# Attention and mixer kernel: the last part put in program order instead of the scheduler's order

## The chip, the cores and the metric

The kernel runs on one core of a Trainium2 chip. A core has five engines that each work through a queue of their own and wait for each other by semaphores: TensorE (PE, with the weight loads shown apart as PEld), VectorE (DVE), ScalarE (ACT), GpSimd (POOL) and SyncE (SP). DMA queues move data between the device's memory and the core. The metric is the device time of one execution in microseconds (us).

## The reference

Inputs are `q`, `k`, `v` (8 batches, 8 heads, 576 positions, 64 elements), `s` (8, 8, 576), and the weights `U` (576 x 32), `V` (32 x 576), `w_ch1` (512 x 2048) and `w_ch2` (2048 x 512). All is float32; the kernel works in bfloat16 with float32 sums.

```python
scores = scale * np.matmul(q, k.transpose(0, 1, 3, 2))
cum = np.cumsum(np.maximum(s, 0.0), axis=-1)
bias = -(cum[:, :, :, None] - cum[:, :, None, :])
scores = np.where(causal, -1000000000.0, scores + np.minimum(bias, 0.0))
attn = softmax(scores)                       # over the last axis
x = np.matmul(attn, v)                       # heads side by side: (8, 576, 512)
h = x.transpose(0, 2, 1) @ U @ V             # low-rank mixing along the sequence
u = x + h.transpose(0, 2, 1)
out = u + np.maximum(u @ w_ch1, 0.0) @ w_ch2
```

## The kernel before

The 64 pairs of batch and head are taken two heads at a time: 32 head pairs n = 0 to 31, four to a batch. For one head pair there are these pieces of work.

- `place(g)` prepares two head pairs (group g): DVE turns the loaded `qk_sd` by four transposes (line 172), and SP issues one DMA for the bias rows (line 164) and eight for the turned data (line 177) into one of three slots. It stands two head pairs ahead of the scores that use it.
- `scores(n)` multiplies k and q on PE (line 205), 18 matmuls into seven score tiles, ACT takes the exponential (lines 219, 227, 231, 235), and DVE cuts the part above the diagonal by a minimum with a mask (line 198). The bias is in the matmul, by four more rows of q and k.
- `values(n)` multiplies by v for each of the two heads (15 matmuls, line 261); DVE then takes the reciprocal of the row sums (line 270) and multiplies into the tile `x_sb` (line 271).
- `mix(n)` is the sequence mixer. Five matmuls with U (line 286) write columns 0 to 127 of the tile `up`; DVE casts them to `ux` (line 295). Four matmuls (line 298) and one (line 306) copy x in transposed form by an identity, and two (lines 315 and 318) add V times `ux`. Line 306 writes columns 128 to 191 of `up`, the tile that line 295 reads. DVE copies the sums into `uT` (lines 326 and 327).
- `widen(g)` and `narrow(g)` are the two halves of the FFN over 512 tokens. A step of `widen` is four matmuls of 512 columns (line 339) and a RELU on ACT (line 346). A step of `narrow` is four matmuls of 512 columns (line 355); each fourth step adds four matmuls that add u (line 366), a copy of the sum on DVE (line 375) and a DMA to the output (line 376).

The FFN steps are a list, `fill`. `run(gen, rate)` takes a piece of work from one `yield` to the next and after each takes `rate` steps from the list. `attend(n, rate)` runs `scores(n)`, `values(n - 1)` and `mix(n - 1)` in this way: four, two and one yields. So the text of the program has an FFN step after each part of the scores, after each head of `values`, and after the first ten matmuls of `mix`.

`opening()` does batch 0, `second()` batch 1 with a rate of 0.4, and `rest()` the other batches with a rate of 1.0, then the FFN steps that are left. Nothing is in the list during `attend(8)`: `widen(1)` is put into it after that pair.

The order in which each engine meets its instructions is set in two ways. Within `tc.manual_schedule()` it is the order of the program's text. Outside it, the framework's own scheduler orders the instructions of each engine by priorities and by what it expects to be ready, and it may pull an instruction ahead of others that the program has first. `opening()` and `second()` lie within, `rest()` outside.

Matmul results go to two pools of four PSUM tiles: `ps_s` for scores, `ps_w` for all others. `qk_sd` has three buffers, `turned` and `x_sb` two, `o_sb` three.

Of the kernel before, what the change touches and what calls it, by code (L numbers as in the profile page):

```python
# [20 lines left out]
def kernel(  # L21
# [81 lines left out]
    def load_qk(g):  # L103
        qk_t[g] = loads.tile([128, 2, ST * D], BF16, tag="qk_sd", name="qk_sd", bufs=3)
        for c, src in enumerate((q, k)):
            for a in range(4):
                nc.gpsimd.dma_start(  # L107
                    out=qk_t[g][ds(32 * a, 32), c, :].rearrange("p (n f) -> p n f", n=6),
                    in_=src[g // 2, 4 * (g % 2) + a].rearrange("(n p t) d -> p n (t d)", p=32, t=3),
                )  # L110

    def load_v(b):
        vt = v_slots[b % 3]
        for t in range(4):
            nc.gpsimd.dma_start(  # L115
                out=vt[:, t, :, 0:D],
                in_=v[b, :, ds(t * 128, 128), :].rearrange("h p d -> p h d"),
            )
        nc.gpsimd.dma_start(
            out=vt[:64, 4, :, 0:D], in_=v[b, :, 512:576, :].rearrange("h p d -> p h d")  # L120
        )
# [40 lines left out]
    def place(g):  # L162
        slot = slots[g % NSLOT]
        nc.sync.dma_start(
            out=slot[D:KA, :, 0 : 2 * S],
            in_=rows_hbm[:, ds(4 * g, 4)].rearrange("r n c s -> r n (c s)"),
        )
        src = qk_t.pop(g)
        turned = work.tile([128, 2, 2, S], BF16, tag="turned", name="turned")
        for e in range(2):  # L170
            for c in range(2):
                nc.vector.transpose(  # L172
                    turned[:, e, c].rearrange("p (n m t) -> p n t m", n=6, t=3),
                    src[:, c].rearrange("p (n t e d) -> p e n t d", n=6, t=3, e=2)[:, e],
                )
            for a in range(4):
                nc.sync.dma_start(
                    out=slot[ds(32 * e, 32), a, 0 : 2 * S],
                    in_=turned[ds(32 * a, 32), e].rearrange("p c s -> p (c s)"),
                )  # L180
# [153 lines left out]
    def widen(g):  # L334
        hT = hidden[g] = work.tile([128, NF, 512], BF16, tag="hT", name="hT")
        for nf in range(NF):
            f1 = pwork()
            for kt in range(4):
                nc.tensor.matmul(  # L339
                    f1,  # L340
                    lhsT=w1_sb[nf // 4][:, kt, ds(nf % 4 * 128, 128)],
                    rhs=uT[:, kt, ds(g * 512, 512)],
                    start=(kt == 0),
                    stop=(kt == 3),
                )
            nc.scalar.activation(hT[:, nf, :], f1, RELU)  # L346
            yield

    def narrow(g):
        hT = hidden.pop(g)  # L350
        for i in range(4):
            f2 = pwork()
            tok = g * 512 + i * 128
            for nf in range(NF):
                nc.tensor.matmul(  # L355
                    f2,
                    lhsT=hT[:, nf, ds(i * 128, 128)],
                    rhs=w2_sb[nf // 4][:, nf % 4, :],
                    start=(nf == 0),
                    stop=False,  # L360
                    skip_group_check=True,
                )
                if nf % 4 == 3 and nf < NF - 1:
                    yield
            for dt in range(4):
                nc.tensor.matmul(  # L366
                    f2[:, ds(dt * 128, 128)],
                    lhsT=uT[:, dt, ds(tok, 128)],
                    rhs=identity,
                    start=False,  # L370
                    stop=(dt == 3),
                    skip_group_check=True,
                )
            o_sb = work.tile([128, DM], FP32, tag="o_sb", name="o_sb", bufs=3)
            nc.vector.tensor_copy(o_sb, f2)  # L375
            nc.sync.dma_start(out=out_flat[ds(tok, 128), :], in_=o_sb)
            yield
# [4 lines left out]
    def step_fill():  # L382
        while fill:
            if next(fill[0], fill) is not fill:
                return
            fill.pop(0)
# [19 lines left out]
    def attend(n, rate):  # L406
        b, hp = divmod(n, PB)
        if n < NP:
            run(scores(n), rate)
        if n > PB:  # L410
            run(values(n - 1), rate)
            run(mix(n - 1), rate)
            if hp == 0:
                fill.append(widen(b - 1))
# [117 lines left out]
    def second():  # L532
        fill.append(widen(0))
        place(2)
        fill_with(6)
        load_qk(4)
        load_v(2)
        for i in range(3):
            load_w2(i)
        load_qk(5)  # L540
        load_w2(3)
        attend(4, 0.4)
        place(3)
        attend(5, 0.4)
        attend(6, 0.4)
        place(4)
        attend(7, 0.4)
        fill_with(16)

    def rest():  # L550
        for n in range(2 * PB, NP + 1):
            b, hp = divmod(n, PB)
            if hp == 0 and b + 1 < B:
                load_qk(2 * b + 2)
                load_qk(2 * b + 3)
                load_v(b + 1)
            if hp % 2 == 0 and n // 2 + 1 < NP // 2:
                place(n // 2 + 1)
            attend(n, 1.0)
            if n == 2 * PB:  # L560
                fill.append(narrow(0))
            if hp == 0:
                fill.append(narrow(b - 1))
        fill.append(widen(NG - 1))
        fill.append(narrow(NG - 1))
        while fill:
            step_fill()

    with tc.manual_schedule():
        opening()  # L570
        second()
    rest()


# [28 lines left out]
```

## Time and profile before

| | |
|---|---|
| median of 3 runs | 425.99 us (425.75 to 426.89) |
| the profiled execution | 425.99 us, of which span 423.9 us |
| PE busy | 386.5 us (91%) |
| DVE, ACT, POOL busy | 198.2, 191.9, 111.4 us |
| mean granted PE clock | 0.954 |
| HBM read, written | 37.51 MB, 9.95 MB |

The span is the time from the first to the last instruction of the program; the execution takes some 2 us more around it. "Busy" is the time that an engine has an instruction in work. A matmul is drawn for longer than it holds the next one back, so PE can look busy while it waits a little. A line of a timeline has its start, its length, the engine, the line of the program, the operation, what it writes and reads, how many instructions are merged, and in brackets the engine's idle time before it with what ended that.

### The profile page before, as it was taken

What the parts mean: (1) busy time and instruction counts of PE and PEld (TensorE: products, weight loads), DVE (VectorE), ACT (ScalarE), POOL (GpSimd) and SP (SyncE); (2) the same over time, 40 slices, a digit from 0 to 9 for tenths busy, and PEclk for the clock granted to TensorE, in tenths of its full rate; (3) what the DMA queues carried; (4) which work ended last, traced back from release to release, by engine and by line L of the source; (5) the groups of instructions that cost most, each with busy time, mean ns of one, the idle gap of its engine ahead of it and who ended that gap; (6) DMA issues with size and microseconds to landing.
All of it is one profiled execution on the core that took longest, in us unless ns stands there. A gap on an engine that the chain in (4) does not pass through costs nothing.

```text
span 423.9 us, 8293 instructions
## 1 busy us (share of the span) xinstructions
PE 386.5 (91%) x3252; PEld 220.4 (52%) x3308; DVE 198.2 (47%) x433; ACT 191.9 (45%) x375; POOL 111.4 (26%) x179
## 2 busy tenths in 40 slices
PE   6794786769999999999999999999999999999996
PEld 2473343545555556555555655566555444444442
DVE  7565443779667685655747443344434101001011
ACT  3362463645652334773376337743770260440620
POOL 8566753295851850620030000000000000000000
PEclk9579868988999999999999999999999999999999
DMA  7999999899993996892291221001000201102001
GB/s 112 155 139 111 198 157 193 114 179 159 170 128 108 193 154 124 85 103 79 64 120 29 73 65 56 2 26 51 26 2 25 76 0 51 49 0 76 26 26 74
DMA packets 78573, 37.93 MB, mean 89 GB/s; under 512 B 64518, under 2 KB 69798, under 8 KB 78534
## 3 DMA queue, kind: packets, MB, share of 16 engines
q0 software_dynamic: 67312, 18.44, 52.7%
q1 hardware_dynamic: 11222, 18.96, 15.3%
q8 instruction: 26, 0.43, 0.4%
q14 instruction: 13, 0.11, 0.1%
HBM read 37.51 MB, written 9.95 MB: 112 GB/s over the span
## 4 chain that ended last, share of the span: by engine, by line
PE 65%; DMA 19%; POOL 6%; DVE 4%; issue 3%; SPq 1%; DVEq 0%; POOLq 0%
PE pwork L355 26%; PE pwork L339 23%; DMA w_sb<-in_moe_w_ch_dram 6%; PE pscore L205 6%; DMA v_slot<-in_v_dram 5%; PE pwork L261 4%; DMA qk_sd<-in_k_dram 4%; DMA qk_sd<-in_q_dram 3%; DVE turned L172 3%; POOL qk_sd L107 3%; PE pwork L286 2%; PE pwork L366 2%; POOL v_slot L115 2%; PE pwork L315 1%; DMA slot<-turned 1%
## 5 line engine op out<-in xcount | busy, mean ns | idle before, releaser
L339 PE MATMUL pwork<-uT,w_sb 128*128 128x512 bf16 x548 | 143.8, 390 | 1.8 <-issue 0.4
L355 PE MATMUL pwork<-w_sb,hT 128*128 128x512 bf16 x552 | 138.1, 379 | 1.2
L346 ACT ACTIVATE hT<-pwork 128x512 bf16<-128x512 f32 x144 | 87.7, 610 | 112.3 <-PE pwork L339 112.2
L205 PE MATMUL pscore<-slot 68*128 68x128 bf16 (+4 forms) x576 | 71.8, 254 | 10.9 <-DMA slot<-turned 6.4
L339 PEld LDWEIGHTS <-w_sb 128*128 128x128 bf16 x576 | 52.5, 100 | 52.4 <-issue 7.7
L355 PEld LDWEIGHTS <-hT 128*128 128x128 bf16 x576 | 51.3, 97 | 47.8 <-issue 1.8
L219 ACT ACTIVATE pT<-pscore 128x512 bf16<-128x512 f32 x64 | 38.8, 606 | 76.1 <-PE pscore L205 62.4
L375 DVE COPY o_sb<-pwork 128x512 f32<-128x512 f32 x36 | 24.8, 689 | 96.7 <-PE pwork L366 96.6
L205 PEld LDWEIGHTS <-slot 68*128 68x128 bf16 x576 | 44.9, 104 | 43.0 <-issue 12.7
L172 DVE STREAM_TRANSPOSE turned<-qk_sd 128x576 bf16<-128x576 bf16 x56 | 58.6, 1116 | 0.8 <-DMA slot<-turned 0.4
L198 DVE TENSOR_TENSOR pT<-pT,keep 128x512 bf16<-128x512 bf16 (+1 forms) x84 | 27.4, 350 | 48.7 <-ACT pT L219 44.4
L227 ACT ACTIVATE pT<-pscore 128x512 bf16<-128x512 f32 x64 | 39.0, 610 | 12.0 <-PE pscore L205 11.9
L261 PEld LDWEIGHTS <-pT 128*128 128x128 bf16 x960 | 37.4, 99 | 11.6 <-issue 0.2
L107 POOL DMA_DIRECT2D qk_sd<-in_q_dram x56 | 31.7, 580 | 32.4 <-DVE pT L198 19.5
L261 PE MATMUL pwork<-v_slot,pT 128*128 128x65 bf16 x960 | 40.0, 195 | 0.0
L115 POOL DMA_DIRECT2D v_slot<-in_v_dram x32 | 28.2, 898 | 42.9 <-PE pwork L261 42.0
L231 ACT ACTIVATE pT<-pscore 128x512 bf16<-128x512 f32 x64 | 39.4, 616 | 0.0
L107 POOL DMA_DIRECT2D qk_sd<-in_k_dram x56 | 31.6, 573 | 26.0 <-DMA w_sb<-in_moe_w_ch_dram 13.2
L326 DVE CAST uT<-pwork 128x512 bf16<-128x512 f32 x31 | 21.3, 688 | 23.4 <-PE pwork L318 23.4
L271 DVE TENSOR_TENSOR x_sb<-pwork,rec 128x320 bf16<-128x320 f32 x64 | 31.2, 488 | 1.9
L286 PE MATMUL pwork<-x_sb,U_sb 128*128 128x128 bf16 x160 | 14.6, 223 | 13.4 <-DVE x_sb L271 13.3
L270 DVE RECIPROCAL rec<-pwork 128x5 f32<-128x5 f32 x64 | 12.0, 188 | 26.3 <-PE pwork L261 26.2
(61 smaller groups left out, 186.7 us busy)
## 6 DMA issues: line engine op xcount, KB each, us to landing
out_dram<-o_sb SPq DMA_DIRECT2D x36, 256.0 KB
slot<-turned SPq DMA_DIRECT2D x112, 72.0 KB
v_slot<-in_v_dram POOLq DMA_DIRECT2D x32, 128.0 KB, 6.4
w_sb<-in_moe_w_ch_dram POOLq DMA_DIRECT2D x8, 512.0 KB, 8.2
qk_sd<-in_q_dram POOLq DMA_DIRECT2D x56, 72.0 KB, 5.5
qk_sd<-in_k_dram POOLq DMA_DIRECT2D x56, 72.0 KB, 4.4
v_slot<-in_v_dram POOLq DMA_DIRECT2D x8, 64.0 KB, 7.0
rows_hbm<-hT SPq DMA_DIRECT2D x1, 504.0 KB
```

The costliest lines, as they stand in the source:

```text
L107: nc.gpsimd.dma_start(out=qk_t[g][ds(32 * a, 32), c, :].rearrange("p (n f) -> p n f", n=6), in_=src[g // 2, 4 * (g % 2) + a].rearrange("(n ...
L115: nc.gpsimd.dma_start(out=vt[:, t, :, 0:D], in_=v[b, :, ds(t * 128, 128), :].rearrange("h p d -> p h d"),)
L172: nc.vector.transpose(turned[:, e, c].rearrange("p (n m t) -> p n t m", n=6, t=3), src[:, c].rearrange("p (n t e d) -> p e n t d", n=6, t= ...
L205: nc.tensor.matmul(dst, lhsT=kT[:, ds(j * 128, 128)], rhs=qT[:, lo:hi], start=start, stop=stop, skip_group_check=not stop,)
L219: nc.scalar.activation(pT[:, hh, 0:512], diag, EXP, scale=scale)
L227: nc.scalar.activation(pT[:, hh, 512:1024], far, EXP, scale=scale)
L231: nc.scalar.activation(pT[:, hh, 1024:1536], mid, EXP, scale=scale)
L261: nc.tensor.matmul(po[:, i, :], lhsT=pT[:, hh, ds(spot(j, i), 128)], rhs=vt[:, j, h, :], start=(j == 0), stop=(j == i), skip_group_check=True,
L271: nc.vector.tensor_tensor(x_sb[:, :, ds(h * D, D)], po[:, :, 0:D], rec.to_broadcast([128, 5, D]), op=ALU.mult,)
L339: nc.tensor.matmul(f1, lhsT=w1_sb[nf // 4][:, kt, ds(nf % 4 * 128, 128)], rhs=uT[:, kt, ds(g * 512, 512)], start=(kt == 0), stop=(kt == 3),)
L346: nc.scalar.activation(hT[:, nf, :], f1, RELU)
L355: nc.tensor.matmul(f2, lhsT=hT[:, nf, ds(i * 128, 128)], rhs=w2_sb[nf // 4][:, nf % 4, :], start=(nf == 0), stop=False, skip_group_check=True,
```

## The change

The call of `rest()` is moved into the block of `tc.manual_schedule()`. All instructions of batches 2 to 7 and of the FFN after them then stand on every engine in the order of the program's text. No instruction is added, removed or altered.

```diff
     with tc.manual_schedule():
         opening()
         second()
-    rest()
+        rest()
```

## The prediction

> **What bounds the kernel now.** I read the page's busy times first, then busy time by stretch, then the tensor engine's (PE's) timeline around one mixer step, and last the vector engine's (DVE's) where PE waits longest.
>
> ```profile
> PE 386.5 (91%) x3252; PEld 220.4 (52%) x3308; DVE 198.2 (47%) x433; ACT 191.9 (45%) x375; POOL 111.4 (26%) x179
> PE   6794786769999999999999999999999999999996
> ```
>
> PE is the bound. Its idle time lies in the first quarter, up to about 106 us. Busy time by stretch (columns: us, then busy time of PE, PEld, DVE, ACT, POOL with instruction counts, granted clock, DMA, GB/s) says the same:
>
> ```profile
> 83.30:104.00 20.70, 14.94 (x127) 8.96 (x126) 18.05 (x35) 9.21 (x20) 14.12 (x23) 0.84 1.60 165
> 100.00:326.00 226.00, 221.44 (x2115) 131.41 (x2153) 127.49 (x294) 117.44 (x234) 49.91 (x79) 1.00 0.58 84
> 326.00:420.00 94.00, 93.53 (x472) 44.33 (x478) 9.68 (x14) 28.66 (x48) 0.00 (x0) 1.00 0.11 40
> ```
>
> From 100 us on PE has almost nothing to win: the reader should see 221.4 of 226 us and, in the tail, 93.5 of 94. So a new order of the same instructions can win only what is left of waits, and loses whatever PE waits it opens. Busy time hides part of a wait, because a matmul is drawn longer than its issue distance (512 columns are drawn 0.38 us and follow each other every 0.215). I therefore count a wait as the distance between two starts less the usual distance. PE's timeline around three mixer steps (start, us, what, idle before):
>
> ```profile
> 174.42 1.03 PE L339 MATMUL pwork<-uT,w_sb 128*128 128x512 bf16 x4
> 175.28 0.22 PE L205 MATMUL pscore<-slot 68*128 68x128 bf16 x1
> 175.41 0.45 PE L286 MATMUL pwork<-x_sb,U_sb 128*128 128x128 bf16 x5
> 175.70 0.39 PE L298 MATMUL pwork<-identity,x_sb 128*128 128x128 bf16 x4
> 175.93 0.38 PE L339 MATMUL pwork<-uT,w_sb 128*128 128x512 bf16 x1
> 176.25 0.19 PE L306 MATMUL pwork<-identity,x_sb 128*128 128x64 bf16 x1
> 176.28 0.81 PE L339 MATMUL pwork<-uT,w_sb 128*128 128x512 bf16 x3
> ...
> 194.38 0.45 PE L286 MATMUL pwork<-x_sb,U_sb 128*128 128x128 bf16 x5
> 194.67 0.39 PE L298 MATMUL pwork<-identity,x_sb 128*128 128x128 bf16 x4
> 195.22 0.19 PE L306 MATMUL pwork<-identity,x_sb 128*128 128x64 bf16 x1 [0.16 <-DVE ux L295]
> ```
>
> L306 writes into the tile that the cast L295 still reads, so it waits for that cast. Where L306 follows L298 at once it starts 0.55 us after it instead of 0.23: a wait of 0.32. Where the scheduler put one FFN matmul between (175.93), L306 starts 0.32 after that one instead of 0.215: a wait of 0.107.
>
> **The change, part by part.** Nothing is added or removed; every instruction from batch 2 on is put in the order in which `rest()` issues it. I compared the two built programs' orders. On PE, before, each of the 24 mixer steps of pairs 8 to 31 mostly stands as nine matmuls (five L286, four L298), FFN matmuls, L306, FFN matmuls, L315 and L318, with one score matmul or an extra FFN matmul ahead of L286. After, all 24 stand as ten in a row, then one FFN step, then L315 and L318, with just one FFN step between the last L261 and L286.
>
> *L306.* Before, in the stretch from 100 to 326 us: 15 of the 24 wait 0.107, two 0.32, one 0.36, one 0.205, five nothing: 2.8 us. After: the ten in a row put all 24 at 0.32 or more. For five pairs (10, 14, 18, 22, 26) a FFN output tile ends in the step just before L286, and the DVE order then is L375 (its copy), then L295. L375 starts 0.20 after the last L366, holds the next DVE instruction back 0.60 and L306 starts 0.34 after L295 starts: 1.14, of which the nine matmuls cover 0.51; 0.63 is left. So 19 x 0.323 + 5 x 0.63 = 9.3. That is **+6.5**. Bounds: -0.2 if every one waits only the 0.107 of the row at 175.93, +8.8 if the five wait 1.1 each. I take the bare row, because all 24 will stand as it does.
>
> *L286 waits for x_sb (L271).* From 100 us on these waits add up to 3.5 us before; 2.6 of it are four long ones (0.40, 0.55, 1.35, 0.32) behind a transpose L172 or copy L375 that the scheduler placed among L270 and L271. After, no L172 stands there. But only one FFN step covers reciprocal and multiply: at 315.93 such a step is followed by L286 0.98 later, 0.863 of it work, a wait of 0.12. 19 such pairs give 2.3 (in the other five the step has four L366 more and covers all).
> The four L172 of a `place` now stand together ahead of the pair's L198, L270. From the end of L318: 0.17 to the copies, 0.71 for L326 and L327, 4 x 0.98 for L172, 0.8 for three L198: the first L270 can start at 5.6 us. PE needs 1.37 for the scores, 4 x 0.86 for FFN steps, 0.45 for L261 and 0.23 to DVE: 5.5. The second L270 is due 1.3 later, so the lateness is made good; with one or two L375 (0.6 each) ahead of it some 0.5 us in all remain. Sum 2.8: **-0.7**. Bounds: -3.5 (all such waits gone) to +6 (0.6 more in each of 10 pairs with `place` in this stretch, less what went).
>
> *The start of `rest()`, 83 to 104 us.* DVE there, before:
>
> ```profile
> 84.85 0.18 DVE L270 RECIPROCAL rec<-pwork 128x5 f32<-128x5 f32 x1
> 84.95 1.09 DVE L172 STREAM_TRANSPOSE turned<-qk_sd 128x576 bf16<-128x576 bf16 x1
> 85.89 0.48 DVE L271 TENSOR_TENSOR x_sb<-pwork,rec 128x320 bf16<-128x320 f32 x1
> 86.27 0.19 DVE L270 RECIPROCAL rec<-pwork 128x5 f32<-128x5 f32 x1
> 86.37 1.09 DVE L172 STREAM_TRANSPOSE turned<-qk_sd 128x576 bf16<-128x576 bf16 x1
> 87.30 0.47 DVE L271 TENSOR_TENSOR x_sb<-pwork,rec 128x320 bf16<-128x320 f32 x1
> ...
> 87.83 0.72 PE L286 MATMUL pwork<-x_sb,U_sb 128*128 128x128 bf16 x5 [4.33 <-DVE x_sb L271]
> ```
>
> Two transposes of `place(5)` were pulled up into the middle of this chain, and PE waits 4.33 us. After, they stand behind L327, so L286 can start at about 86.0 (1.8 earlier). Next, scores(8) needs the slot that `place(4)` fills. Its last L177 is issued at 86.7, as now; at the two earlier places scores began 3.8 and 4.0 us after the last L177, so 90.6, against 91.19 now. Then the gain is lost again: pair 8 has no FFN step to fill with, since widen(1) is queued only after it. So 0.9 for L261, bare, waits for DVE, where `place(5)`'s L172 run from 88.9 to 92.8 and L198 waits for the last exponential (about 94.2): L286 of pair 7 at about 95.9 against 97.34. Before, the scheduler had by then also done scores(9) (1.37 us). Up to L261 of pair 8 come 0.85 + 0.25 for the mixer, 1.37 for scores(9), 3.45 for four FFN steps: 101.8. Before it starts at 103.93 with nine more matmuls of scores(10) done (0.68), so 103.25 like for like: a gain of 1.4 if the clock stays full, 0 if another 3.4 us go at half clock. I take **-0.8**; bounds 0 and -2.7 (slots land by 88.8, full clock).
>
> The clock rows of this stretch:
>
> ```profile
> 84.40:87.80 3.40, 0.00 (x0) 0.00 (x0) 3.40 (x10) 0.00 (x0) 3.28 (x6) 1.00 0.86 138
> 87.80:91.20 3.40, 3.14 (x16) 1.81 (x18) 2.16 (x3) 0.27 (x1) 3.10 (x6) 0.50 1.27 195
> 94.70:98.10 3.40, 2.44 (x22) 1.60 (x23) 3.40 (x9) 3.26 (x8) 1.10 (x3) 0.99 2.69 148
> 98.10:101.50 3.40, 3.40 (x14) 1.59 (x14) 3.40 (x8) 0.00 (x0) 1.09 (x2) 0.50 1.99 155
> ```
>
> A wholly idle 3.4 us is followed by 3.4 us at 0.50, but so is a stretch with PE drawn busy 2.44 of 3.4 us. The Trainium skill (TensorE: Matmul & The Clock Gate, Part 1) has the clock halved after one idle window of about 3.4 us. By that rule none of the new waits (2.6 us at most) would halve it, this step would be -1.4 instead of -0.8 and the sum 430.4; the row at 98.1 speaks against relying on it.
>
> *Other queues.* SP's copies L376 now stand ahead of the `place` that follows them in the program; each waits for a L375 that is ahead of that place's L172 on DVE too, so SP holds nothing up. Slots: L172 done 5 us into a pair, eight L177 at 0.6, 4 to land: 14 us, and the slot is wanted two pairs (19 us) later. POOL's order is the same but for one load of v, six pairs before its use; its loads start later, as qk_sd comes free later, with some six pairs in hand. ACT needs about 7 us of each 9.5. The last 94 us have the same order in both. All cost nothing unless a pair's time fell to 14/2 = 7 us.
>
> **Sum.** 6.5 - 0.7 - 0.8 = +5.0 us. The profiled execution took 425.99 us, its span 423.9 and 2.1 around it; it is also the median of the three shown. Forecast **431.0 us** (+1.2%).
>
> **Rivals.**
> 1. *Faster: the freed DVE chain outweighs.* The long x_sb waits go (4.33 at 83.3 and the four later ones). Priced at its best: -2.7 at the start, -3.5 at L286. It decides only if the L306 waits come to less than 6.2 us more, under 0.375 each; at 0.215 each (+2.4) the time is 426.0 + 2.4 - 6.2 = 422.2. Against it: the trace has seven bare places at full clock, each with 0.32. 6%.
> 2. *Four L172 in a row make every second pair late.* If L198 and L375 between them push L270 past 1.3 us of slack, each of ten pairs loses 0.6 more, +6: 437. For it: DVE has 7.6 us of work in such a pair of 9.5. Against: the slack above. 10%.
> 3. *No change that shows.* Start at -2.7 and L306 at +4 (the five without their copy, some more hidden): 426 to 427.3. 6%. That the change does nothing is excluded, the orders differ on PE from pair 8 on.
>
> **How the numbers follow.** My forecast's case, 428 to 434, has 78%. A measurement here tells about 0.3% (1.3 us) from no change. The low end takes the start at -2.7, L286 at -1.4 and the five copies at no cost (-1.5): +0.9 to +1.4, so 427.4; the high end adds 3.5 of rival 2's 6 us: 434.5. Faster 6%, within 0.3% 6%, slower 88%.
>
> **What would show it.** In the profile after: L306's group waits for ux in 20 or more places, 0.16 us each as drawn; the waits of L286 over 1 us gone after 100 us; L286 of pair 6 near 86 us; PE's busy share unchanged in the last 94 us; span near 429. Wrong would be: L306 not waiting (then rival 1), or DVE idle-free in every second pair with L286 waiting 0.5 us and more (rival 2).

## The result and the profile after

| | median | ratio to before, 95% interval |
|---|---|---|
| before | 425.87 us | |
| after | 431.9 us | 1.013 (1.0092 to 1.0168) |
| after, measured again later | 432.11 us (before: 426.05) | 1.0126 (1.009 to 1.0161) |

The change makes the kernel 6 us slower, between 4 and 7 by the interval; 5.0 were forecast. The profiled execution of after took 429.94 us (span 428.2), the fastest of its four, against 423.9 of span before. Its first 82 us, which hold the same instructions in both kernels, happened to be 1.0 us quicker. Counted from the second head of pair 6's values (the L261 at 82.88 before, 81.90 after) to the end it is 341.1 us before and 346.3 after: 5.2 us more, like for like.

The page of after, busy times and PE in 40 slices, then busy time by stretch:

```profile
PE 387.3 (90%) x3251; PEld 219.3 (51%) x3308; DVE 198.7 (46%) x433; ACT 191.8 (45%) x375; POOL 111.4 (26%) x179
PE   6695796659999999999999999999999999999996
```

```profile
83.30:104.00 20.70, 14.23 (x145) 9.13 (x148) 12.04 (x31) 9.58 (x20) 13.20 (x21) 0.92 1.39 142
100.00:326.00 226.00, 218.45 (x2088) 128.76 (x2126) 129.20 (x294) 117.95 (x237) 48.20 (x76) 1.00 0.53 82
330.00:424.00 94.00, 93.47 (x471) 44.38 (x479) 9.69 (x14) 28.66 (x48) 0.00 (x0) 1.00 0.11 40
```

The work is the same, instruction by instruction. In the stretch from 100 to 326 us PE is busy 3 us less and so gets less done; the last 94 us are as before. The 40 slices hide it, since each still shows a 9: what was lost is many small waits. PE's timeline around two mixer steps shows the two sizes that they have:

```profile
113.85 0.45 PE L286 MATMUL pwork<-x_sb,U_sb 128*128 128x128 bf16 x5
114.14 0.39 PE L298 MATMUL pwork<-identity,x_sb 128*128 128x128 bf16 x4
114.68 0.19 PE L306 MATMUL pwork<-identity,x_sb 128*128 128x64 bf16 x1 [0.16 <-DVE ux L295]
114.71 1.02 PE L339 MATMUL pwork<-uT,w_sb 128*128 128x512 bf16 x4
...
123.30 0.39 PE L366 MATMUL pwork<-identity,uT 128*128 128x128 bf16 x4
123.52 0.44 PE L286 MATMUL pwork<-x_sb,U_sb 128*128 128x128 bf16 x5
123.80 0.39 PE L298 MATMUL pwork<-identity,x_sb 128*128 128x128 bf16 x4
124.66 0.19 PE L306 MATMUL pwork<-identity,x_sb 128*128 128x64 bf16 x1 [0.48 <-DVE ux L295]
```

At 114 us L306 starts 0.54 us after the first L298 where four such matmuls take 0.22: 0.32 us lost. At 123.5 us it starts 0.86 after: 0.64 lost. DVE's timeline says why the second is longer: the copy L375 stands ahead of the cast L295 that L306 waits for.

```profile
123.72 0.69 DVE L375 COPY o_sb<-pwork 128x512 f32<-128x512 f32 x1 [0.36 <-PE pwork L366]
124.33 0.28 DVE L295 CAST ux<-pwork 128x128 bf16<-128x128 f32 x1
```

Among all waits this is one line (us in total, times, longest us). Before had the first of these two, after has the second, with four times as much:

```profile
PE pwork L306 <- DVE ux L295: 1.5, 9, 0.2
PE pwork L306 <- DVE ux L295: 6.5, 31, 0.5
```

Measured as starts less usual distance, pairs 8 to 31 lose 19 x 0.32 and 5 x 0.64 us here, 9.3 in all.

At the start of `rest()` the transposes no longer split the chain of pair 6. PE there:

```profile
85.27 0.45 PE L286 MATMUL pwork<-x_sb,U_sb 128*128 128x128 bf16 x5 [2.75 <-DVE x_sb L271]
...
87.24 0.86 PE L205 MATMUL pscore<-slot 68*128 68x128 bf16 x9
88.33 1.36 PE L205 MATMUL pscore<-slot 68*128 68x128 bf16 x9 [0.24 <-ACT pT L219]
89.53 1.08 PE L261 MATMUL pwork<-v_slot,pT 128*128 128x65 bf16 x30
94.19 0.61 PE L286 MATMUL pwork<-x_sb,U_sb 128*128 128x128 bf16 x5 [3.58 <-DVE x_sb L271]
```

The wait of 4.33 us is 2.75 now. But pair 7, which has no FFN step to fill with, waits 3.58 us for DVE, which does `place(5)`'s four transposes first:

```profile
88.15 4.02 DVE L172 STREAM_TRANSPOSE turned<-qk_sd 128x576 bf16<-128x576 bf16 x4
92.02 0.85 DVE L198 TENSOR_TENSOR pT<-pT,keep 128x512 bf16<-128x512 bf16 x3
...
93.64 0.49 DVE L271 TENSOR_TENSOR x_sb<-pwork,rec 128x320 bf16<-128x320 f32 x1
```

### The profile page after: what moved, and what is told of

Its sections match the earlier page's. It is cut to its first block, busy times and chain, and to the rows that moved or that the text cites. A ratio compares the mean times of both kernels' runs of the same rounds, so it can differ in the third digit from the quotient of the medians.

```text
span 428.2 us, 8269 instructions
## 1 busy us (share of the span) xinstructions
PE 387.3 (90%) x3251; PEld 219.3 (51%) x3308; DVE 198.7 (46%) x433; ACT 191.8 (45%) x375; POOL 111.4 (26%) x179
## 4 chain that ended last, share of the span: by engine, by line
PE 73%; DMA 15%; DVE 5%; POOL 4%; issue 2%; SPq 0%; DVEq 0%; POOLq 0%
PE pwork L355 28%; PE pwork L339 26%; PE pscore L205 8%; DMA w_sb<-in_moe_w_ch_dram 7%; PE pwork L261 5%; DMA hT<-in_k_dram 2%; PE pwork L366 2%; PE pwork L286 2%; DMA slot<-turned 2%; DMA v_slot<-in_v_dram 2%; DVE ux L295 2%; POOL v_slot L115 1%; DVE turned L172 1%; DMA qk_sd<-in_q_dram 1%; DVE o_sb L375 1%
## 5 line engine op out<-in xcount | busy, mean ns | idle before, releaser
L355 PE MATMUL pwork<-w_sb,hT 128*128 128x512 bf16 x549 | 136.7, 379 | 1.4
L205 PE MATMUL pscore<-slot 68*128 68x128 bf16 (+4 forms) x576 | 69.9, 253 | 11.7 <-DMA slot<-turned 6.3
L375 DVE COPY o_sb<-pwork 128x512 f32<-128x512 f32 x36 | 24.8, 688 | 97.4 <-PE pwork L366 97.4
L172 DVE STREAM_TRANSPOSE turned<-qk_sd 128x576 bf16<-128x576 bf16 x56 | 56.5, 1115 | 0.2 <-issue 0.2
L261 PEld LDWEIGHTS <-pT 128*128 128x128 bf16 x960 | 37.2, 99 | 11.4
L261 PE MATMUL pwork<-v_slot,pT 128*128 128x65 bf16 x960 | 39.5, 195 | 0.0
L271 DVE TENSOR_TENSOR x_sb<-pwork,rec 128x320 bf16<-128x320 f32 x64 | 31.5, 492 | 2.2
L286 PE MATMUL pwork<-x_sb,U_sb 128*128 128x128 bf16 x160 | 14.6, 222 | 12.4 <-DVE x_sb L271 12.2
L286 PEld LDWEIGHTS <-U_sb 128*128 128x128 bf16 x160 | 9.5, 98 | 22.0 <-DVE x_sb L271 17.9
```

What stands on the lines that cost most here:

```text
L172: nc.vector.transpose(turned[:, e, c].rearrange("p (n m t) -> p n t m", n=6, t=3), src[:, c].rearrange("p (n t e d) -> p e n t d", n=6, t= ...
L205: nc.tensor.matmul(dst, lhsT=kT[:, ds(j * 128, 128)], rhs=qT[:, lo:hi], start=start, stop=stop, skip_group_check=not stop,)
L261: nc.tensor.matmul(po[:, i, :], lhsT=pT[:, hh, ds(spot(j, i), 128)], rhs=vt[:, j, h, :], start=(j == 0), stop=(j == i), skip_group_check=True,
L286: nc.tensor.matmul(up[:, 0:128], lhsT=U_sb[:, t, :], rhs=x_sb[:, t, cols], start=(t == 0), stop=(t == 4), skip_group_check=True,)
L355: nc.tensor.matmul(f2, lhsT=hT[:, nf, ds(i * 128, 128)], rhs=w2_sb[nf // 4][:, nf % 4, :], start=(nf == 0), stop=False, skip_group_check=True,
```

## The experiments

Each edit is shown against the kernel named. Times are medians. The kernel before, run beside each session, took 425.67 us with E1 to E4, 425.65 with E5 to E8 and 426.05 with E9 to E11.

Single executions of one kernel lie some us apart, and much of that arises in the first 100 us. The long stretch can be compared more sharply: from the first L286 of pair 8 to the end of the span, where the granted clock is 1.00 in all these profiles up to the last microsecond. After and its repetition E10 agree there within 0.1 us, though their spans are 2.4 us apart.

| kernel | L286 of pair 8 starts | span | from there to the end |
|---|---|---|---|
| after | 104.28 | 428.2 | 323.9 |
| E10, after again | 106.69 | 430.6 | 323.9 |
| E1 | 107.53 | 422.1 | 314.6 |
| E3 | 103.31 | 427.2 | 323.9 |
| E4 | 110.60 | 442.5 | 331.9 |
| E5 | 107.38 | 422.0 | 314.6 |
| E6 | 105.42 | 418.2 | 312.8 |
| E7 | 109.37 | 431.4 | 322.0 |
| E8 | 104.64 | 426.6 | 321.9 |

### E1 and E2: L306 ahead of L286

```diff
         up = pwork()
+        if n >= 2 * PB:
+            tail_of_x()          # the matmul of line 306, start=True
         for t in range(5):
             nc.tensor.matmul(up[:, 0:128], ..., start=(t == 0), ...)
...
-        nc.tensor.matmul(up[:, 128:192], lhsT=x_sb[:, 4, cols], ..., start=True, ...)
+        if n < 2 * PB:
+            tail_of_x()
```

E1 does this to after, E2 to before. The cut is shortened: `tail_of_x()` is a function that holds the one matmul of line 306.

> Kernel after, with the matmul of L306 issued ahead of the five of L286 for pairs 8 to 31 (in the code: for n >= 8). Theory (the wait of L306 for the cast L295 is the loss): 24 such waits, 9.3 us in the profile of after, are gone; the next to need the cast is L315, 1.39 us after the first of the ten, and the cast is done by 1.14 at the latest, so no new wait; L286's waits for x_sb stay as they are. Span 428.2 - 9.3 = 419, time 431.9 - 9.3 = 422.6 us, faster than before (0.992). Rival (the pairs are paced by the vector engine's chain, and PE only meets the next wait): under 3 us less, 429 us or more.

> Kernel before (scheduler's order in the last part), with the same move of L306. Theory: only the 2.8 us that such waits cost in before can go: 425.9 - 2.8 = 423.1 us (0.993), so that with and without the scheduler the kernel is within 1 us once this wait is gone. Rival (the scheduler's order is worth more than that elsewhere): this kernel is faster than the one with program order by 3 us or more, 419 to 420 us.

In both kernels a part of the computation is lost and the output is another one. The likely reason is that a start flag of L286 now comes behind L306 on the same tile, so that x of the last 64 positions of a batch does not reach u (last section). The number and size of the instructions are the same.

E1: **422.86 us**, 0.9934 (0.9911 to 0.9957), where 422.6 was expected. No wait of L306 for the cast is left, and the waits for x_sb, now at the moved matmul, are as in after (2.5 us from 100 us on). From L286 of pair 8 to the end the profile is 9.3 us shorter than after, which is the sum of the waits that were taken away. The loss of the change is this wait; nothing else takes its place.

E2: 423.68 us, 0.9955 (0.9924 to 0.9985), expected 423.1. So far with and without the scheduler look alike once the wait is gone: from the second head of pair 6's values to the end both profiles have 338.6 us. Of these the granted clock was 0.50 for 13.7 us in E1 and for 6.8 in E2, so this agreement says little of the order itself; E11 comes back to it.

### E3: `place(5)` behind pair 8

```diff
-            if hp % 2 == 0 and n // 2 + 1 < NP // 2:
+            if n > 2 * PB and hp % 2 == 0 and n // 2 + 1 < NP // 2:
                 place(n // 2 + 1)
             attend(n, 1.0)
+            if n == 2 * PB:
+                place(n // 2 + 1)
```

> Kernel after, with place(5) issued after head pair 8's work instead of ahead of it. Theory (place(5)'s four L172 hold x_sb of pair 7): L286 of pair 7 starts near 92.2 us instead of 94.2, since only the last exponential and L198 stand before it; 1.9 us gained there. The slot for scores(10) then lands at 102.5 to 105 us, and scores(10) is due at 102.7, so up to 2.3 us are given back there: time 430 to 432 us. Rival (the wait at pair 7 has another cause, such as the exponentials or the clock): L286 of pair 7 stays at 93.7 us or later.

429.66 us, 1.0093 (1.0058 to 1.0128): 2.2 less than after, but the two intervals overlap. The profile is clearer. In it the distance from L286 of pair 6 to L286 of pair 7 is 7.19 us where after has 8.92, 1.7 less, near the 1.9 of the theory; from L286 of pair 8 on it is as long as after. PE:

```profile
87.40 0.45 PE L286 MATMUL pwork<-x_sb,U_sb 128*128 128x128 bf16 x5 [2.74 <-DVE x_sb L271]
...
94.59 0.44 PE L286 MATMUL pwork<-x_sb,U_sb 128*128 128x128 bf16 x5 [1.86 <-DVE x_sb L271]
...
105.27 0.42 PE L205 MATMUL pscore<-slot 68*128 68x128 bf16 x5
```

scores(10) at 105.27 waits for nothing, so the part that was to be given back was not. The absolute times that were expected are missed by 2 us, since this execution reached pair 6 that much later. In this execution the clock gained too. After, the stretch behind the wait of 3.58 us ran at half clock, here the stretch behind a wait of 1.86 us did not (columns as above; the first two rows are after, the third is E3):

```profile
90.90:94.30 3.40, 0.11 (x2) 0.11 (x2) 3.17 (x9) 0.00 (x0) 3.40 (x7) 1.00 2.17 163
94.30:97.70 3.40, 3.18 (x20) 2.05 (x20) 1.54 (x4) 0.60 (x1) 1.63 (x4) 0.50 2.21 141
```

```profile
94.60:98.00 3.40, 3.24 (x29) 2.02 (x29) 2.44 (x5) 1.58 (x4) 0.06 (x1) 1.00 1.65 97
```

That is not the edit's doing for sure. E6 below has the same edit and the same wait of 1.86 us, and in its profile the stretch behind it did run at half clock (the wait lies in the first row):

```profile
93.28:96.69 3.41, 1.39 (x18) 1.01 (x18) 1.98 (x7) 0.31 (x3) 0.79 (x2) 1.00 2.10 126
96.69:100.10 3.41, 3.41 (x11) 1.42 (x10) 3.41 (x6) 2.15 (x4) 0.00 (x0) 0.50 0.05 1
```

The Trainium skill (TensorE: Matmul & The Clock Gate, Part 1) has the clock halved after one idle window of about 3.4 us. The rows of after and of E3 agree with that. E6's row, with PE busy for 1.39 us, does not, and neither does the prediction's row at 94.70. So the measurements go beyond that rule, and what decides the clock after a short wait stays open.

### E4: one more transpose in each place

```diff
-            for c in range(2):
+            for c in ([0]*1 if e == 0 and g > 4 else []) + [0, 1]:
                 nc.vector.transpose(turned[:, e, c]..., src[:, c]...)
```

> Kernel after, with one of the four transposes L172 of each place from place(5) on done twice (the output is the same). It takes 0.98 us more on the vector engine in each of 11 places. In after the second L270 of such a pair waits 0.42 us for PE where no L375 stands ahead of it, and not at all where one does. Theory (that is all the slack there is): 0.56 us more in about five pairs, 0.98 in about five, 0.98 in pair 8: +8 us, 440 us. Rival (the four transposes are well covered, as the forecast had it with 1.3 us of slack): +1 to +2, 433 to 434 us.

442.28 us, 1.039 (1.0348 to 1.0432): 10.4 over after, more than the 8 of the theory and far from the 1 to 2 of the forecast's cover. From L286 of pair 8 to the end the profile is 8.0 us longer than after, close to the 7.7 that the theory has for the ten pairs there. The rest lies ahead of that, where the granted clock was 0.50 for 10.2 us in this execution and for 3.4 in after. In its timeline DVE runs without a break from the copies to the second L271 of a pair with a copy, and PE waits:

```profile
133.58 5.22 DVE L172 STREAM_TRANSPOSE turned<-qk_sd 128x576 bf16<-128x576 bf16 x5
138.66 0.72 DVE L198 TENSOR_TENSOR pT<-pT,keep 128x512 bf16<-128x512 bf16 x2
139.30 0.68 DVE L375 COPY o_sb<-pwork 128x512 f32<-128x512 f32 x1
...
140.88 0.49 DVE L271 TENSOR_TENSOR x_sb<-pwork,rec 128x320 bf16<-128x320 f32 x1
```

```profile
141.42 0.45 PE L286 MATMUL pwork<-x_sb,U_sb 128*128 128x128 bf16 x5 [0.87 <-DVE x_sb L271]
```

The four transposes fit in after, but only just: of the 0.98 us of a fifth some 0.2 are covered in the mean of the ten pairs.

### E5: the wait taken away with the computation kept

```diff
             nc.tensor.matmul(up[:, 0:128], ..., start=(t == 0), ...)
+        nc.tensor.matmul(
+            up[:, 128:192], lhsT=x_sb[:, 4, cols], rhs=identity[:, :64],
+            start=False, stop=False, skip_group_check=True,
+        )
         ux = work.tile([128, 128], BF16, tag="ux", name="ux")
         nc.vector.tensor_copy(ux, up[:, 0:128])
...
-        nc.tensor.matmul(up[:, 128:192], ..., start=True, stop=False, ...)
```

> Kernel after, with L306 issued right behind the five matmuls of L286 and ahead of the cast L295, without a start flag of its own (the one of L286 opens the tile for it), in every pair. Theory: the same 9.3 us as in the run with L306 ahead of L286 go from pair 8 on, and a few tenths before; 422 to 423 us, ratio to before 0.992. Rival (that run was quicker because a part of the computation was lost, not because of the wait): 428 us or more.

**422.9 us**, 0.993 (0.9904 to 0.9956): the same as E1, and 314.6 us from L286 of pair 8 on as there, so E1's time does not come from what it lost. PE's timeline, where L294 is the moved matmul and L306 now the four that were L298; this is the step that waited 0.64 before:

```profile
125.76 0.39 PE L366 MATMUL pwork<-identity,uT 128*128 128x128 bf16 x4
125.98 0.44 PE L286 MATMUL pwork<-x_sb,U_sb 128*128 128x128 bf16 x5
126.26 0.19 PE L294 MATMUL pwork<-identity,x_sb 128*128 128x64 bf16 x1
126.29 0.39 PE L306 MATMUL pwork<-identity,x_sb 128*128 128x128 bf16 x4
126.51 1.03 PE L355 MATMUL pwork<-w_sb,hT 128*128 128x512 bf16 x4
```

With this one matmul moved, program order is faster than both kernels of the case.

### E6 and E7: two FFN steps ahead of the mixer

```diff
                 op=ALU.mult,
             )
-            yield
+            if n < 2 * PB or hh == 1:
+                yield
+            if n >= 2 * PB and hh == 1:
+                yield
```

E7 is after with this edit alone; E6 has it together with those of E5 and E3.

> The kernel of the run before, with two more edits: place(5) behind pair 8's work, and from pair 8 on both FFN steps of the values part behind its second head, so that two steps and not one cover reciprocal and multiply ahead of L286. Theory (terms add up): 422.9 - 2.2 (place(5)) - 2.5 (19 waits of 0.12 and two of 0.26 at L286) = 418.2 us, ratio 0.982. Rival (PE then meets a wait that they hid, such as for a PSUM tile): 421 us or more.

> Kernel after, with only the second of these edits: from pair 8 on both FFN steps of the values part stand behind its second head. Theory: L286's waits after 100 us (2.5 us in the profile of after) go, L306's stay: 429.4 us. Rival (they are a part of the same chain and come back at L306): no change, 431 to 432 us.

E7: 429.96 us, 1.0104 (1.0063 to 1.0145), 1.9 under after, 2.5 expected. The intervals overlap, but the profile is 1.9 us shorter from L286 of pair 8 on. There L286 waits in one place only, 0.08 us, and L306 as in after (19 times 0.32, 5 times 0.64). The two waits are separate. A part of the gain is lost at a new wait. These are all of PE's waits from 100 us on that show as idle time (L309 is what was L306):

```profile
PE pwork L309 <- DVE ux L298: 5.4, 24, 0.5
PE pwork L261 <- DVE uT L329: 0.3, 1, 0.3
```

E6: **418.9 us**, 0.9842 (0.9808 to 0.9876), expected 418.2. The terms add up: E5's time less what E3 and E7 gained (2.2 and 1.9) is 418.8. From 100 us on PE hardly waits:

```profile
100.00:316.00 216.00, 215.68 (x2134) 129.83 (x2133) 128.44 (x296) 118.60 (x237) 52.69 (x84) 1.00 0.58 90
```

### E8: the copy of the FFN's sums on ACT

```diff
-            nc.vector.tensor_copy(o_sb, f2)
+            nc.scalar.copy(o_sb, f2)
```

> Kernel after, with the copy of the FFN's sums (L375) on the scalar engine in place of the vector engine. Theory: the five waits of 0.64 at L306, where that copy stands ahead of the cast, become 0.32, and the two of 0.26 at L286 become 0.12: 1.9 us less, 430 us. Rival (another reason for the five): they stay at 0.64.

428.88 us, 1.0075 (1.0048 to 1.0101), 3.0 under after, 1.9 expected; from L286 of pair 8 on the profile is 2.0 us shorter, so the rest is within the spread. All 24 waits of L306 are 0.32 now, the step with L366 among them, which settles what the five were:

```profile
123.65 0.39 PE L366 MATMUL pwork<-identity,uT 128*128 128x128 bf16 x4
123.88 0.44 PE L286 MATMUL pwork<-x_sb,U_sb 128*128 128x128 bf16 x5
124.16 0.39 PE L298 MATMUL pwork<-identity,x_sb 128*128 128x128 bf16 x4
124.70 0.19 PE L306 MATMUL pwork<-identity,x_sb 128*128 128x64 bf16 x1 [0.16 <-DVE ux L295]
```

### E9 to E11: the scheduler once more

E9 is before with E5's edit, E10 is after unchanged, E11 is E6 with `rest()` outside the manual schedule:

```diff
         second()
-        rest()
+    rest()
```

> Kernel before (scheduler's order in the last part), with L306 right behind the five of L286 and no start flag of its own, the whole computation kept. Theory: 2.8 us of waits at L306 go, as in the run with L306 ahead: 423 to 424 us (0.995). Rival (the earlier run was quicker for the part of the computation that it lost): 425.9 us, no change.

> Kernel after, unchanged, in the same session as the other two, since its four runs lay 2.7 us apart. Theory: 431 us, 1.2% above before; if the median were under 430, the gains put on place(5), on the two steps and on the copy would be smaller by that much.

> The kernel with all three edits, but with rest() outside the manual schedule, in the scheduler's hands. Theory (once the waits are gone the two orders differ only at the start of rest(), where the scheduler pulls transposes into the chain of pair 6 but does scores(9) early): within 1.5 us of the 418.9 us with program order. Rival (the scheduler's order costs something of its own in the long stretch): 421 us or more.

E10 gave 432.11 us, so the comparisons with after stand. The other two went against the theory. E9: 426.33 us, 0.9987 (0.9959 to 1.0015), where 423 to 424 was expected: no gain that can be told. (Its interval overlaps E2's, so that it gains less than E2 is not certain either.) E11: 423.12 us, 0.9924 (0.99 to 0.9948), 4.2 over the 418.9 of the same edits in program order, where at most 1.5 was expected. There the rival held: the scheduler's order costs something of its own.

E9's profile is of the slowest of its twelve executions (430.15 us), so it does not explain the median. It shows one thing that can eat the gain: with the new order of the matmuls the scheduler also made a new order on DVE, with two transposes ahead of the cast (L303 here).

```profile
139.42 2.09 DVE L172 STREAM_TRANSPOSE turned<-qk_sd 128x576 bf16<-128x576 bf16 x2 [1.44 <-DMA slot<-turned]
141.37 0.26 DVE L303 CAST ux<-pwork 128x128 bf16<-128x128 f32 x1
```

```profile
141.69 0.39 PE L315 MATMUL pwork<-V_sb,ux 128*128 128x512 bf16 x1 [2.00 <-DVE ux L303]
```

The first of them waits 1.44 us for DMAs that still read its buffer, the cast waits behind it, and L315 waits 2.0 us for the cast; from 143.1 to 146.5 us the granted clock is 0.50. How much of this the other executions have was not seen, so why E9 gains nothing stays open.

E11's profile is 3.5 us longer than E6's from the second head of pair 6's values to the end. Of this 0.9 lie ahead of the L286 of pair 8: the wait of 4.3 us for x_sb at pair 6 is still there, where E6 waits 2.75 at pair 6 and 1.86 at pair 7. The other 2.6 lie behind it, where PE sits idle at the matmuls of L286 and L315 in five places up to 136 us, 0.2 to 0.9 us each and 2.35 in all, and E6 in none. That accounts for most of it, but no run took these waits away alone, so for E11 the cause is argued and not shown.

## Why the prediction was right, and where it was not

The forecast was 431.0 us, slower with 88%; 431.9 was measured, within the range of 427.4 to 434.5.

- **L306, +6.5 forecast.** Shown: 9.3 us of waits after against 2.8 before, in the two sizes forecast (0.32, and 0.64 where 0.63 had been worked out). E1 and E5 take 9 us away with the wait, 9.3 from L286 of pair 8 on, E8 the part that the copy adds.
- **L286, -0.7 forecast.** 2.5 us after against 3.5 before: -1.0. 19 waits are there, 17 of 0.11 to 0.13 and two of 0.26 behind a copy; E7 removes them. The four long waits behind a transpose or a copy are gone.
- **L172 in a row: the sum was right, its reason too hopeful.** The step let the first L270 be up to 1.3 us late. It took the second L270 as free until PE is done, and left out that it also has to follow the first L271, which takes 0.64 us from the first L270 on. What is left was measured in after as 0.42 us in a pair without a copy, and nothing in one with it; E4 makes it visible. Rival 2 was nearer than its 10% said.
- **The start of `rest()`, -0.8 forecast.** From the second head of pair 6 to L261 of pair 8 before took 21.05 us, less 0.68 for the nine matmuls done early, and after 19.62: -0.75. That the number came out is luck, since two parts of the working were wrong and cancel. scores(8) was said to wait for its slot until 90.6; it began at 87.24 without a wait. And the wait that follows was put at 2.6 us at most, with the clock taken half way between kept and halved; it was 3.58 us, and the clock was halved for 3.4 us. E3 shows that 1.7 us of this wait are `place(5)`.
- **Other queues, nothing.** Shown by the last 94 us and by the absence of a DMA among PE's waits from 100 us on. In E3 even a place one head pair later kept no score waiting.
- **Sum.** +6.5 - 1.0 - 0.75 = +4.75; like for like the profile has +5.2 (and E10's has the same), so 0.4 us are not assigned. The low end of the range was written as +1.4; its own terms give +0.9. And 0.3% was too little for the spread of single executions: before alone ran from 423.65 to 428.14 us beside E1 to E4.
- **Rival 1 and rival 3** needed cheaper waits at L306. None was under 0.32 us at full clock, and their mean, 0.39, lies above the 0.375 of rival 1, which also needed gains of 6.2 us elsewhere where 1.75 came.

## What to carry to other kernels

A small wait that a scheduler hides by putting other work into it is a defect of the program's text: look where one instruction reuses a tile that another engine still reads, and move that instruction ahead of the read. Price a change of order by the distance between starts on the bound engine, since busy shares and the 40 slices show waits of 0.3 us hardly at all, and ask of each queue how much lateness it can make good, one instruction after the other. Here the order by hand lost to the scheduler by 6 us as it stood, and won by 4 once three places were mended.

## What the runs showed of the hardware that was not expected

The start flag seems to reach further than the columns that a matmul writes. In E1 a matmul with start on columns 0 to 127 came after one that had written columns 128 to 191 of the same tile, and the kernel's output was another one; in E5 the later matmul has no start flag of its own, stands behind the one with the flag, and the output is kept. The runs do not show which sums changed in E1. The Trainium skill says what fits (PSUM — Partial Sum Buffer, The four PSUM rules): the flag clears the record of what was written over a whole bank. It also explains why E5's L306 needs no flag, as L286's has just cleared the bank for it.
